# A planned kernel gets new durations, another start of its idle matmuls, a smaller fill of V, and nine of its last residual additions on ScalarE and GpSimd

## The chip, the cores and the metric

The kernel runs on one core of one Trainium2 chip, as one program with one launch. The metric is the device time of that core in microseconds (us); times are medians of several runs. A traced execution also gives the span, from the first to the last instruction, which is a little shorter than its time. The engines are TensorE (PE; its weight loads are listed apart as PEld), VectorE (DVE), ScalarE (ACT), GpSimd (POOL) and SyncE (SP), which here only issues transfers (DMAs).

## What is computed

Four blocks in a row act on a residual stream of 2048 tokens by 512 features, with 32 heads of 16: A, B, A, B, with the same weights for both A and for both B. Each block is `x = x + block(layernorm(x)) @ wo`.

```python
def A(x):                     # causal attention in 4 segments of 512 tokens, with a memory
    for s in range(4):
        p = softmax(q_s @ k_s.T / 4 + causal mask)
        a_mem = phi(q_s) @ M / (phi(q_s) @ z)
        o_s = g * a_mem + (1 - g) * (p @ v_s)
        M, z = M + phi(k_s).T @ v_s, z + sum(phi(k_s))
def B(x):                     # linear attention over all tokens, not causal
    phi_q = concat(softmax(q @ w_phi), softmax(-q @ w_phi))
    phi_k = concat(softmax(k @ w_phi), softmax(-k @ w_phi))
    o = phi_q @ (phi_k.T @ v) / (phi_q @ sum(phi_k))
```

## The kernel before

X, the residual stream, stays in SBUF as 16 tiles of 128 tokens by 512 features, in bf16; so do all weights. A segment, and likewise a chunk of block B, is four tiles. For every segment the kernel does: layernorm (`ln`, statistics by bn_stats and bn_aggr on DVE, the power −1/2 on POOL, L996 to L1006), transposes of the normalized tiles (by DMA from the SP queue, L780, or by PE and a copy, L796, at the start, at the change of layers and at the end), projections (`a_proj`), attention (`a_att`: scores on PE, an exponential of 128x1024 on ACT at L1188, the causal mask on POOL at L1192, PV on PE), output projection and residual (`a_out`, `residual` at L1230), and then the keys and queries of block B for the same tokens (`b_keys`, `b_queries`). Block B's output (`b_out`, L1326) needs all four chunks of its keys, so it comes after the layer's last segment: chunk by chunk between the segments of the next layer, and for the last layer at the very end, where each tile of X goes to HBM as it is done (L1362).

The order of all of this isn't written out by hand. Each step is recorded as an operation (`Program.add`) with its engine or engines to choose from, a cost in us, a latency until others see its result, the operations it depends on, and a priority. `PLAN` (L43 to L180) is a long list that gives every operation its priority by number. `Program.schedule` then plays a clock: at each step it takes, for the engine that can begin first, the ready operation with the lowest priority number, grants it buffers and PSUM banks, and so fixes five queues. `finalize` issues each queue in that order, with waits on semaphores. The chip then runs the five queues in order, with waits only for what an instruction needs. Where the real durations differ from those of the plan, the order stays as planned.

Names and lines that the change and the prediction touch:

- `BEGIN`, `LANDS`, `TO_PE`, `HOP` (L28 to L35): when the engines and loads begin, and how long a result takes to the next engine, in the plan. `BOTH` (L36): the planned time of two score operations that run side by side on different rows of PE. `act_cost` (L730), and the `lat` of `pe`, `act` and `transposed` (L749, L763, L798).
- Idle matmuls (L517 to L551, L578, L1431): where the plan sees a gap on PE, it fills it with matmuls of 128x256 on a tile of zeros, `warm` (filled on DVE at L895), whose results nobody reads. In the plan each lasts 0.108 us, and none begins before 1.5 us. `idle_op` gives each group a dependency on the fill of `warm`.
- `zero_keys` (L953): fills on DVE at the start. Four `Vt` buffers get ones throughout (128x544); V's 16 values per head later overwrite all but every 17th column, which stays one and sums the keys. Four `kt` buffers get zeros.
- The loads at the start: rows of X and halves of WA_k, WA_v, WA_q from the ACT and SP queues, then larger ones from SP (L885 to L951).
- `b_out` with `store` (L1326): per tile a product with Rkv on PE, the denominator and the scaling on DVE (L1345 to L1347), a transposition, the product with `WB_o`, and the residual. In ten of the last sixteen tiles the residual is a DVE addition from PSUM (L1230). In six, named by `TAIL_A` (L1374), PE adds X by a matmul with the identity, and ACT copies the sum to X. `TAIL_T` names the tiles that PE transposes; the others go by a DMA transpose from SP.

Of the kernel before, what the change touches and what calls it, by code (L numbers as in the profile page):

```python
# [8 lines left out]
ALU = mybir.AluOpType  # L9
# [24 lines left out]
BEGIN = 0.75  # L34
LANDS = 2.3  # L35
BOTH = 0.24  # L36
# [212 lines left out]
class Program:  # L249
# [100 lines left out]
    def schedule(self):  # L350
# [137 lines left out]
        while done < n_ops:  # L488
# [26 lines left out]
            (t, _, i, g), e = choice  # L515
            op = ops[i]
            if e == "pe" and self.idle:  # L517
                unit, begin = self.idle[1], self.idle[3]
                recent = [x for x in recent if x[1] > t - WIN]

                def gap(op, t):
# [208 lines left out]
def act_cost(n):  # L730
    return n * 0.000833 + 0.051
# [6 lines left out]
class Kernel:  # L738
# [131 lines left out]
    def gen(self):  # L870
        return self.PS.tile(self.genkind)
# [607 lines left out]
```

## Time and profile before

| what | value |
|---|---|
| median of 3 runs | 515.78 us (515.72, 515.78, 516.08) |
| time of the profiled execution | 514.65 us |
| its span | 512.9 us |
| PE busy, matmuls | 493.3 us (96%), 7314 instructions |
| PEld busy | 304.4 us (59%) |
| DVE busy | 438.2 us (85%), 1026 |
| ACT busy | 436.2 us (85%), 592 |
| POOL busy | 263.1 us (51%), 387 |
| idle matmuls (L1433) | 148, 21.6 us |
| HBM traffic | 6.32 MB read, 2.10 MB written |

A row of a group gives line, engine, operation, output and inputs with their shapes, the count, the total busy time and the mean in ns, and then the idle time of the engine just before it with what ended it. Matmuls overlap: a mean of 380 ns for a 512-wide matmul is its time through the array, while the next one starts about 0.215 us later, so a busy PE isn't PE at its peak, and idle matmuls count as busy. ACT instructions overlap by their ends too: 1078 ns is the mean of the 128x1024 exponential, but they follow each other every 0.92 us.

The span has these stages: the opening to about 20 us; layer 0's four segments, with ACT nearly full, to about 210; the change of layers to about 262, where ACT is at little more than half; layer 1's segments to about 460; and the tail, which has the last keys and queries and the output of the last block B.

### The profile page before, as it was taken

The page shows a single profiled execution, that of the slowest core. Times are in us where ns is not written, and L with a number is a line of the kernel's source. Part 1 is how long each engine was busy: PE and PEld are TensorE (multiplying, and loading weights), DVE is VectorE, ACT ScalarE, POOL GpSimd, SP SyncE. Part 2 cuts the span into 40 slices and gives each one's busy share as a digit, 9 for nine tenths or more (in the row PEclk, how much of TensorE's full clock was granted, in tenths as well). Part 3 has the DMA queues.
Part 4 walks back from the last instruction along what each step waited for, and adds up shares of the span by engine and source line. Part 5 has one row for each costly group of instructions (what it writes and reads, how often), then busy time and mean ns, then how long its engine had stood idle before and what let it go on. Part 6 is the DMA issues. An engine that isn't in the chain of part 4 may idle for free.

```text
span 512.9 us, 17078 instructions
## 1 busy us (share of the span) xinstructions
PE 493.3 (96%) x7314; PEld 304.4 (59%) x7314; DVE 438.2 (85%) x1026; ACT 436.2 (85%) x592; POOL 263.1 (51%) x387
## 2 busy tenths in 40 slices
PE   7999999999999999999999999999999999999997
PEld 6755555665567556657755555565564666565664
DVE  6899789988679978799886998998998678888995
ACT  2999999999999999953599898999999999995433
POOL 4476585545477856240146457565964485732100
DMA  7964423432301311100113534323443222020034
GB/s 250 278 92 79 69 55 52 80 46 43 63 4 26 64 23 23 26 4 4 22 22 65 63 42 87 62 42 60 58 64 63 34 50 38 13 36 5 7 102 123
DMA packets 94539, 29.97 MB, mean 58 GB/s; under 512 B 86272, under 2 KB 94464, under 8 KB 94464
## 3 DMA queue, kind: packets, MB, share of 16 engines
q1 hardware_dynamic: 93216, 27.83, 29.6%
q8 instruction: 58, 0.95, 0.8%
q10 hardware_dynamic: 1248, 1.06, 0.7%
q14 instruction: 17, 0.14, 0.1%
HBM read 6.32 MB, written 2.10 MB: 16 GB/s over the span
## 4 chain that ended last, share of the span: by engine, by line
PE 43%; ACT 41%; DVE 14%; DMA 1%; issue 1%
PE PS L718 39%; ACT PT L1188 32%; ACT Ek L1250 3%; PE PS L1433 3%; ACT phi L1016 2%; DVE stats L996 2%; DVE X L1230 2%; ACT EQ L1299 2%; DVE EQ L1321 1%; PE PS L796 1%; DMA xnT<-xn 1%; DVE O L1347 1%; DVE O L1213 1%; DVE xn L1006 1%; ACT KTo L1299 1%; DVE PhiK L1018 1%
## 5 line engine op out<-in xcount | busy, mean ns | idle before, releaser
L1188 ACT ACTIVATE PT<-PS 128x1024 bf16<-128x1024 f32 x320 | 311.3, 1078 | 12.9 <-PE PS L718 12.2
L1192 POOL TENSOR_SCALAR_AFFINE_SELECT PT<-PT 128x512 bf16<-128x512 bf16 (+2 forms) x280 | 174.6, 635 | 129.6 <-ACT PT L1188 125.8
L718 PEld LDWEIGHTS PS<-VT,PT 128*128 128x128 bf16 x2560 | 75.6, 96 | 19.5 <-POOL PT L1192 2.6
L718 PE MATMUL PS<-VT,PT 128*128 128x17 bf16 x2560 | 82.4, 171 | 1.3 <-DVE stats L996 0.8
L718 PE MATMUL PS<-QT,KT 32*128 32x128 bf16 (+1 forms) x864 | 77.1, 245 | 5.8 <-ACT PT L1188 2.8
L718 PE MATMUL PS<-QT,KTo 32*128 32x128 bf16 (+1 forms) x864 | 75.9, 242 | 2.5 <-ACT PT L1188 1.3
L1255 POOL TENSOR_TENSOR Ek<-Ek,rZ 128x1024 bf16<-128x1024 bf16 x28 | 54.9, 1967 | 37.1 <-DVE rZ L1253 37.0
L718 PEld LDWEIGHTS PS<-QT,KT 32*128 32x128 bf16 x864 | 32.7, 92 | 43.2 <-ACT PT L1188 26.3
L718 PEld LDWEIGHTS PS<-QT,KTo 32*128 32x128 bf16 x864 | 34.9, 93 | 19.8 <-ACT PT L1188 11.7
L1230 DVE TENSOR_TENSOR X<-X,PS 128x512 bf16<-128x512 bf16 x58 | 39.1, 676 | 5.6 <-PE PS L718 5.3
L996 DVE BATCH_NORM_STATS2 stats<-X 128x6 f32<-128x512 bf16 x64 | 43.1, 681 | 0.5
L1250 ACT ACTIVATE Ek<-PS 128x512 bf16<-128x512 f32 x64 | 36.2, 652 | 7.6 <-PE PS L718 7.5
L1251 DVE TENSOR_REDUCE Zk<-Ek 128x64 f32<-128x1024 bf16 x32 | 38.4, 1208 | 3.9 <-ACT Ek L1250 3.6
L1002 POOL TENSOR_TENSOR rstd<-rstd,negh 128x2 f32<-128x2 f32 (+1 forms) x38 | 25.2, 667 | 32.1 <-DVE rstd L1000 30.4
L718 PE MATMUL PS<-xnT,WA_q 128*128 128x128 bf16 x512 | 36.1, 220 | 0.4 <-DVE O L1213 0.4
L718 PE MATMUL PS<-WA_v,xnT 128*128 128x512 bf16 x128 | 36.0, 380 | 0.0
L718 PE MATMUL PS<-WA_k,xnT 128*128 128x512 bf16 x128 | 34.4, 381 | 0.8 <-DVE O L1347 0.4
L718 PEld LDWEIGHTS PS<-xnT,WA_q 128*128 128x128 bf16 x512 | 29.5, 98 | 7.7 <-issue 2.6
L1006 DVE TENSOR_SCALAR xn<-X,mv,rstd 128x512 bf16<-128x512 bf16 x64 | 29.7, 482 | 5.0 <-POOL rstd L1002 4.7
L1213 DVE TENSOR_TENSOR O<-PS,r 128x128 bf16<-128x128 f32 x128 | 31.9, 279 | 1.2
L718 PE MATMUL PS<-WA_o,OT 128*128 128x512 bf16 x128 | 32.5, 380 | 0.1
L718 PE MATMUL PS<-WB_o,OT 128*128 128x512 bf16 x128 | 32.0, 380 | 0.4 <-DVE O L1347 0.3
(132 smaller groups left out, 836.4 us busy)
## 6 DMA issues: line engine op xcount, KB each, us to landing
out_dram<-X SPq DMA_DIRECT2D x16, 128.0 KB, 1.7
X<-in_A_x_dram SPq DMA_DIRECT2D x3, 512.0 KB, 8.6
EQ<-in_B_wqkv_dram SPq DMA_DIRECT2D x2, 512.0 KB, 12.8
OT<-O SPq DMA_TRANSPOSE x46, 2.5
xnT<-xn SPq DMA_TRANSPOSE x36, 2.5
WA_o<-in_A_wo_dram SPq DMA_DIRECT2D x1, 512.0 KB, 10.7
WB_v<-in_B_wqkv_dram SPq DMA_DIRECT2D x1, 512.0 KB, 12.9
WB_o<-in_B_wo_dram SPq DMA_DIRECT2D x1, 512.0 KB, 8.5
```

Of the source, the lines that this page charges most:

```text
L718: return e.matmul(o, l, r, start=st, stop=sp, tile_position=(basep(l), basep(o)))
L996: self.dve(lambda e, t=t: e.bn_stats(self.stats[:, t, :], self.X[:, t, :]), 0.60, [R("X", t)], [R("stats", t)])
L1002: self.pool(lambda e, ve=ve, n=n: e.tensor_tensor(ve, ve, self.negh[:, 0:1].to_broadcast([128, n]), ALU.pow), 0.6, [R("rstd", t0 + i) for ...
L1006: self.dve(lambda e, t=t, xn=xn: e.tensor_scalar(xn.ap[:], self.X[:, t, :], self.mv[:, t, 0:1], self.rstd[:, t:t + 1], op0=ALU.subtract, o ...
L1188: self.act(lambda e, st=st, pt=pt: e.activation(pt.ap[:].rearrange("p b c -> p (b c)"), self.ps[:, st.slot[0] * 512:st.slot[0] * 512 + 102 ...
L1192: self.pool(lambda e, dv=dv, nd=nd: e.affine_select(dv(), dv(), [[0, 2], [0, nd], [1, 128]] if nd > 1 else [[0, 2], [1, 128]], ALU.is_ge, 0.0,
L1213: self.dve(lambda e, r1=r1, view=view, c=c, g=g: e.tensor_tensor(o[c].ap[:, g, :].rearrange("p (h d) -> p h d", d=DH), view()[:, c, :, 0:1 ...
L1230: self.dve(lambda e: e.tensor_tensor(X[:, t, :], X[:, t, :], self.bank(gen), ALU.add), 0.61, [R("X", t), gen()], [R("X", t)])
L1250: self.act(lambda e, sgn=sgn, Ek=Ek, gen=gen: e.activation(Ek.ap[:, sgn, :], self.bank(gen), ACT.Exp, scale=1.0 - 2.0 * sgn), 512, [gen()] ...
L1251: self.dve(lambda e, Ek=Ek, Zk=Zk: e.tensor_reduce(Zk.ap[:], Ek.ap[:].rearrange("p s (h j) -> p s h j", h=H), AX.X, ALU.add), 1.15, [Ek(0) ...
L1255: scale = lambda e, Ek=Ek, rZ=rZ: e.tensor_tensor(Ek.ap[:].rearrange("p s (h j) -> p (s h) j", j=DH), Ek.ap[:].rearrange("p s (h j) -> p ( ...
L1299: self.act(lambda e, sgn=sgn, g=g, gen=gen: e.activation(Eq[sgn].ap[:, g, :], self.bank(gen), ACT.Exp, scale=1.0 - 2.0 * sgn), 512, [gen() ...
```

## The change

The planner's constants and costs are changed, and the list of priorities is a new one of other numbers throughout (not shown). Idle matmuls may begin, in the plan, when the fill of `warm` has ended there, in place of a fixed 1.5 us; and for 3.5 us from then on each counts twice its time. `Vt` is filled in its 17th column alone. In the tail, nine tiles get their residual by an ACT copy from PSUM to a spare `PT` buffer as f32, and a POOL addition to X; DVE keeps six, PE and ACT one.

```diff
-BEGIN = 0.75
+BEGIN = 0.9
+COLD = 3.5
-BOTH = 0.24
+BOTH = 0.27
 PLAN = (
...
-                unit, begin = self.idle[1], self.idle[3]
+                unit, w = self.idle[1], self.idle[2][0]
+                begin = 1e9 if end[w] is None else end[w] + TO_PE["dve"]
+                warmed = begin + COLD
...
-                    return max(0, int((t - at - (SWITCH if op.mode else 0.0) - MARGIN) / unit))
+                    t -= (SWITCH if op.mode else 0.0) + MARGIN
+                    cold = max(0, int((min(t, warmed) - at) / (2 * unit)))
+                    return cold + max(0, int((t - max(at, warmed)) / unit))
+
+                def lasts(at, n):
+
+                    cold = min(n, max(0, int((warmed - at) / (2 * unit))))
+                    return (n + cold) * unit
...
-    return n * 0.000833 + 0.051
+    return n * 0.000833 + 0.063
...
-    def pe(self, mms, reads, writes, pre=(), lat=0.17, cost=None, rows=0):
+    def pe(self, mms, reads, writes, pre=(), lat=0.11, cost=None, rows=0):
...
-        return self.P.add("act", f, act_cost(n), reads, writes, lat=0.13)
+        return self.P.add("act", f, act_cost(n), reads, writes, lat=0.07)
...
-        self.P.add("pe", tr, 0.24, list(reads) + [self.R("ident")], [gen()], lat=0.17, pre=pre)
+        self.P.add("pe", tr, 0.24, list(reads) + [self.R("ident")], [gen()], lat=0.11, pre=pre)
...
-            self.dve(lambda e, b=b: e.memset(b[:], 1.0), 0.25, (), [self.R("vbone")])
+            self.dve(lambda e, b=b: e.memset(b[:, :, 16:17], 1.0), 0.15, (), [self.R("vbone")])
...
-                self.dve(lambda e, b=b: e.memset(b[:], 0.0), 0.25, (), [self.R("ktzero")])
+                self.dve(lambda e, b=b: e.memset(b[:], 0.0), 0.28, (), [self.R("ktzero")])
...
-            self.pool(... ALU.pow), 0.6,
+            self.pool(... ALU.pow), 0.76,
...
-                self.pe(mms, reads, [st()], pre=[pt], lat=0.2, cost=0.23, rows=y + 1)
+                self.pe(mms, reads, [st()], pre=[pt], lat=0.14, cost=0.23, rows=y + 1)
...
-                              0.085 + 0.26 * nd, [pt()], [pt()])
+                              0.176 + 0.23 * nd, [pt()], [pt()])
...
+            elif tt in pool_add:
+                y = self.p_PT.tile()
+                yv = lambda y=y: y.ap[:].rearrange("p a b -> p (a b)").bitcast(F32)
+                self.act(lambda e, yv=yv, gen3=gen3: e.activation(yv(), self.bank(gen3), ACT.Copy), 512, [gen3()], [y()])
+                self.pool(lambda e, yv=yv, t=t: e.tensor_tensor(self.X[:, t, :], self.X[:, t, :], yv(), ALU.add), 1.0, [R("X", t), y()], [R("X", t)])
...
-        TAIL_T, TAIL_A = ((0, 1, 2, 3), (0, 2), (0, 2), (0, 2)), ((3,), (3,), (1, 3), (1, 3))
+        TAIL_T, TAIL_A = ((0, 1, 2, 3), (0, 2), (0, 2), (0, 2)), ((), (), (), (3,))
+        TAIL_P = (1, 3), (1, 2, 3), (1, 2, 3), (1,)
```

As built, the changed kernel's queues stand in another order on every engine. PE's queue begins with 33 idle matmuls in place of 51, then the first transposes, then 8 in place of 6; over the whole kernel there are 131 in place of 148. On DVE's queue the fill of `warm` is fourth in place of sixth. On SP's queue a half of WA_v is ahead of a half of WA_q, and WA_o is ahead of the second segment's rows. Which engine makes a copy out of PSUM changes for some: net, outside the residuals, eight fewer on ACT and eight more on DVE, three of them 256 wide. The last ten of the sixteen outputs stand in one row at the end of SP's queue, in place of the last seven.

More of the change, by code (lines that the diff above doesn't have):

```diff
@@ L544, in schedule @@
                     if banks:
-                        f = self.idle_op(at, n, min(banks)[1])
+                        f = self.idle_op(at, n, min(banks)[1], lasts(at, n))
                         queues[e].append(f.i)
@@ L576, in schedule, with idle_op @@
         return max(end)
-    def idle_op(self, at, n, bank):
-        emit, unit, after, _ = self.idle
+    def idle_op(self, at, n, bank, lasts):
+        emit, unit, after = self.idle
         f = Op()
@@ L583, in idle_op @@
         f.emit = {"pe": lambda e: emit(e, n, bank)}
-        f.cost, f.lat, f.pri, f.weight, f.mode = {"pe": n * unit}, 0.17, 0.0, 1.0, 0
+        f.cost, f.lat, f.pri, f.weight, f.mode = {"pe": lasts}, 0.17, 0.0, 1.0, 0
         f.rows, f.mate = 0, None
@@ L1001, in ln @@
                       [R("mv", t0 + i) for i in range(n)], [R("rstd", t0 + i) for i in range(n)])
-            self.pool(lambda e, ve=ve, n=n: e.tensor_tensor(ve, ve, self.negh[:, 0:1].to_broadcast([128, n]), ALU.pow), 0.6,
+            self.pool(lambda e, ve=ve, n=n: e.tensor_tensor(ve, ve, self.negh[:, 0:1].to_broadcast([128, n]), ALU.pow), 0.76,
                       [R("rstd", t0 + i) for i in range(n)] + [R("negh")], [R("rstd", t0 + i) for i in range(n)])
@@ L1324, in b_queries, with b_out @@
         return Eq, ze
-    def b_out(self, c, Eq, ze, pri0, pri1, store, by_pe=(), add_pe=()):
-        self.P.tag = (self.L, "bout%d" % c)
+    def b_out(self, c, Eq, ze, pri0, pri1, store, by_pe=(), add_pe=(), pool_add=()):
+        self.P.tag = (self.L, ("tail%d" if store else "bout%d") % c)
         R, P = self.R, self.P
@@ L1429, in build @@
                 for c in range(4):
-                    self.b_out(c, *prev[c], base + 90 + c, base + 91 + c, True, by_pe=TAIL_T[c], add_pe=TAIL_A[c])
+                    self.b_out(c, *prev[c], base + 90 + c, base + 91 + c, True, by_pe=TAIL_T[c], add_pe=TAIL_A[c], pool_add=TAIL_P[c])
         def idle(e, n, b):
@@ L1434, in idle @@
             return ins
-        P.idle = (idle, 0.108, [self.R("warm").last_write], 1.5)
+        P.idle = (idle, 0.108, [self.R("warm").last_write])
         P.psum = self.PS
```

272 rows, old and new, of the table PLAN are left out of this document.

## The prediction

> **What bounds the kernel now.** I read the page's chain of waits first, then its first groups, then the opening and the tail in order of time, then busy time by stretch.
>
> The page's chain, by engine:
>
> ```profile
> PE 43%; ACT 41%; DVE 14%; DMA 1%; issue 1%
> ```
>
> PE and ACT take turns in setting the end; a microsecond taken from DVE or POOL is worth little unless it stands in a stage of its own. The busiest group of the page, and the stretches of the two attention stages (columns: stretch, length, then busy us of PE, PEld, DVE, ACT, POOL):
>
> ```profile
> L1188 ACT ACTIVATE PT<-PS 128x1024 bf16<-128x1024 f32 x320 | 311.3, 1078 | 12.9 <-PE PS L718 12.2
> ```
>
> ```profile
> 20.00:200.00 180.00, 174.53 (x2818) 105.52 (x2817) 154.66 (x358) 175.09 (x224) 117.35 (x170) 1.00 0.35 57
> 262.00:460.00 198.00, 191.53 (x3031) 114.27 (x3029) 169.93 (x396) 188.39 (x244) 120.48 (x178) 1.00 0.31 51
> ```
>
> ACT is idle 4.9 us of 180 (2.7%) and 9.6 us of 198 (4.9%): both stages go at ACT's pace, but for these 14.5 us. The opening in order of time (start, us):
>
> ```profile
> 2.85 0.17 DVE L895 MEMSET warm<- 128x128 uint32 x1
> 3.08 7.38 PE L1433 MATMUL PS<-warm 128*128 128x256 bf16 x51 [3.08 <-DVE H8b L907]
> 7.03 0.41 DVE L1006 TENSOR_SCALAR xn<-X,mv,rstd 128x512 bf16<-128x512 bf16 x1
> 10.29 0.39 PE L796 MATMUL PS<-ident,xn 128*128 128x128 bf16 x4
> ...
> 14.01 1.06 PE L718 MATMUL PS<-xnT,WA_q 128*128 128x128 bf16 x16
> ```
>
> This is a stall that PE makes for itself. The first normalized tile is there at 7.44, but the 51 idle matmuls ahead of its transposes last until 10.46. The plan put them from 1.5 on at 0.108 us each, to end at 7.0; they waited for the fill of `warm` (3.02), and went at 4 in 0.5 us until 6.5, the rest at about 0.11 each. The chain of waits begins with this group and goes on over PE's matmuls to 34.3, then over ACT's exponentials; so what is saved here shifts all behind it. What could hold it then are the loads (kind, queue, KB, us to landing):
>
> ```profile
> WA_v<-in_A_wv_dram ACTq DMA_DIRECT2D x1, 256.0 KB, 6.0
> WA_q<-in_A_wq_dram SPq DMA_DIRECT2D x1, 256.0 KB, 7.4
> WA_v<-in_A_wv_dram SPq DMA_DIRECT2D x1, 256.0 KB, 8.6
> WA_q<-in_A_wq_dram ACTq DMA_DIRECT2D x1, 256.0 KB, 8.4
> ```
>
> Issued at 2.21, 2.27, 2.77 and 3.25, they land at 8.2, 9.7, 11.4 and 11.7. The tail, in two stretches (same columns):
>
> ```profile
> 478.00:489.00 11.00, 10.40 (x161) 8.39 (x160) 11.00 (x30) 2.77 (x6) 0.00 (x0) 1.00 0.12 23
> 489.00:510.00 21.00, 21.00 (x178) 12.87 (x178) 18.50 (x45) 7.66 (x13) 0.00 (x0) 1.00 0.41 110
> ```
>
> DVE is full to 489; then PE is, and the chain runs over PE to 510.1, where ACT makes the last tile and its output goes. POOL does nothing.
>
> **The change part by part.**
>
> *Opening: −2.2 us.* V's fill shrinks from 544 to 32 elements (0.51 us each; a 128x32 copy of L925 takes 0.22), and as built only one stands ahead of `warm` in place of two, with two 0.33 us steps of key fills. From 0.91: 0.33 + 0.2 + 0.33, so `warm` begins near 1.8 rather than 2.85 and PE at 2.0. Now 33 idle matmuls follow: 16 in the 3.5 slow us, 17 at 0.11, ending at 7.4. The DVE rows to the first tile don't move: its second bn_stats waits for the second row load (1.24 + 3.6 = 4.9), against 5.23 before, so the tile comes at 7.1 to 7.4. Transposes at 7.4 instead of 10.18: 2.8 us. Of that the loads give back some: the order on SP puts WA_v ahead of WA_q, so V's second half lands about 9.7, Q's about 11.7. After 8 idle matmuls, two transposes, 16 K matmuls and 2 wide ones PE stands at V near 9.9 (not held), and at Q near 11.2, held to 11.7, where before it stood at 14.01: 2.3 us. I take 2.2. Bounds: 2.9 if Q isn't held; 0.5 if the later loads (WA_o now ahead of the next rows on SP, the raw weights) hold the first segment instead. What else moves in SP's queue, the transposes of raw weights and their places among the xnT ones, feeds the second segment, whose first exponentials come some 37 us later (40 tiles at 0.917), and the keys of chunk 0 (58.4). That is the cover.
>
> *Durations and the new order: −0.8 us.* The constants change no instruction, but the order of all five queues and who does a copy. They are nearer to the trace: nine exponentials of the chain take 8.25 us, 0.917 each; planned 0.904, now 0.916. A round from transposes (471.01) over ACT's copy (471.43) to the next matmul (472.11) takes 1.10; the old constants add to 0.24 + 0.20 + 0.478 + 0.29 = 1.21, the new ones to 0.24 + 0.14 + 0.490 + 0.23 = 1.10. That makes the new order likelier to fit; it prices nothing. What can be priced: outside the residuals ACT loses net five 512-wide copies and three 256-wide ones (5 x 0.49 + 3 x 0.28 = 3.3 us; a pair of 512-wide goes by in 0.98), and DVE gets them (5 x 0.61 + 3 x 0.35 = 4.1). By the chain's shares: −3.3 x 0.41 + 4.1 x 0.14 = −0.8. Idle matmuls outside the opening stay (91, then 90). For the bounds: if both attention stages left ACT idle 2.7%, 4.2 us would go; at 4.9% in both, 3.8 would come. I take −0.8, the row nearest to what is known.
>
> *Tail: −1.1 us.* DVE's residuals fall from 10 to 6 (4 x 0.61 = 2.4 us), identity matmuls on PE from 6 to 1 (5 x 0.21 = 1.1 us of the chain's PE). Nine tiles go by an ACT copy (the L774 copies take 0.60, and ACT is busy 7.66 of 21) and a POOL addition. No row shows that addition. Nearest is
>
> ```profile
> L1255 POOL TENSOR_TENSOR Ek<-Ek,rZ 128x1024 bf16<-128x1024 bf16 x28 | 54.9, 1967 | 37.1 <-DVE rZ L1253 37.0
> ```
>
> By elements half of it, 0.98 us; by bytes (3 KB read per partition against 2.25) 2.62. I take the first: it is the same operation, and half as many elements. The added wait: outputs on SP wait for POOL, and all later outputs stand behind. As built, the last 10 outputs follow SP's last transposes, at 0.585 each (7 in 4.09 before), 5.9 us. Take E for the end of PE's last matmul. From the tiles 1 to 3 on, PE still has transposes and matmuls of 6.2 us, so they come near E−5.5 and the last output can go at E+0.7 as it does now. POOL has five additions in that time (tiles 3, 1, 11, 10, 13): at 0.98 they end at E−0.6, unseen; above 1.12 each tenth costs 0.5 us. So only PE's 1.1 us counts. Bounds: −2.5 if the DVE time counts too; +1.0 if the addition takes 1.5 (+1.9, less 1.1, rounded up).
>
> [...]
>
> *Sum.* −2.2 − 0.8 − 1.1 = −4.1. The profiled execution: span 512.9, time 514.65 (1.75 around it). So 510.55 for such an execution; the median shown, 515.78, lies 1.13 above it: **511.7 us**.
>
> **The rivals.**
>
> *The new order fits better than the copies say (0.22).* ACT's idle time falls in both stages to the 2.7% of the first: −4.2 in place of −0.8, so 508.3. For it: the constants that now meet 0.917 and 1.10. Against: by the table of waits PE waits for ACT 109 times before weight loads (41.8 us), and these depend on tiles and banks, not on constants.
>
> *The new order fits worse (0.10).* 4.9% in both: +3.8 in place of −0.8, so 516.3, no change to be told. For it: DVE, full from 230 to 250 (20.0 of 20.0 us), gets two more xnT copies there. Against: these are 1.2 us.
>
> *POOL's additions follow bytes (0.08), slower.* At 2.62 five of them end at 5 x 2.62 − 5.5 = 7.6 behind E, the last outputs 7.5 later: 511.7 + 7.5 = 519.2. It decides from 4.1 us on, so from 1.94 us each. For it: the f32 tile is as large as the 1024-wide bf16 one. Against: that row's broadcast operand shows a cost by element.
>
> *The opening gives nothing (0.10).* The loads of the raw weights and rows take the whole first 20 us (DMA share 0.89): −0.5 in place of −2.2, so 513.4. Against: the four landings above.
>
> **How the numbers follow.** The forecast has 0.50. Repeated measurements of this kernel can tell about 0.2%, 1.0 us. Faster by more: forecast, better fit, opening lost, less 0.05 for what strays out of each: 0.77; within: the worse fit: 0.10; slower: POOL and those 0.05: 0.13. The forecast's own range is 509.5 to 513.5; the better fit pulls down to 507, the worse fit up to 516.6, and POOL by bytes is left out.
>
> **What would show it.** Opening: the first group on `warm` with 33, from about 2.0 to 7.4; transposes at 7.4; the Q matmuls near 11.7; ACT's first exponential at 18.5 rather than 20.65. Middle: nine exponentials still 8.25, ACT idle near 2.7% and 4.9%. Tail: POOL's rows on X near 1.0 us, the last instruction an ACT copy to X, seven or more outputs at 0.585 without a gap. The prediction is wrong if the opening's lead is gone by 100 us, or if POOL's X rows exceed 1.9.

## The result and the profile after

The changed kernel takes **520.00 us** (median of 20 runs, 516.88 to 522.71); the kernel before, run beside it, 515.87. The ratio is 1.0075, 95% interval 1.0058 to 1.0091: 0.75% slower, where 511.7 was forecast. The times are spread over 6 us, and they go with the mean granted clock that each execution records:

| mean clock of the execution | executions of 20 | median us |
|---|---|---|
| 0.999 to 1.0 | 3 | 517.06 |
| 0.996 to 0.997 | 4 | 519.02 |
| 0.983 to 0.990 | 13 | 520.89 |

In the 122 executions of the kernel before that ran beside the experiments, the lowest mean clock is 0.993. So two things are to be explained: some 1.4 us at the full clock (the changed kernel's five such executions, with those of a second series below, have a median of 517.0 us, the kernel before 515.2 to 515.7), and 2 to 4 us more where the clock falls. The profiled execution (517.06 us, span 515.3) has the full clock throughout, so it shows the first alone. Its span is 2.4 us longer than that of the profile before, since that one (514.65 us) is among the faster of its kernel; differences of about 1 us between two traces are within what one kernel shows (executions of the kernel before at the full clock have spans of 512.5 to 514.4 us). Its chain and its busiest group:

```profile
PE 57%; ACT 25%; DVE 10%; DMA 5%; issue 1%; SPq 1%; POOL 0%
...
L1198 ACT ACTIVATE PT<-PS 128x1024 bf16<-128x1024 f32 x320 | 309.0, 1049 | 12.2 <-PE PS L728 11.2
```

ACT's share of the chain fell from 41% to 25%; PE has it now, and transfers (DMA) went from 1% to 5%. The exponentials themselves cost no more (1049 ns against 1078). By stretches (length, then busy us of PE, PEld, DVE, ACT, POOL):

```profile
20.00:200.00 180.00, 170.89 (x2717) 103.12 (x2715) 152.91 (x349) 172.32 (x219) 114.29 (x168) 1.00 0.35 56
262.00:460.00 198.00, 192.12 (x3006) 115.54 (x3006) 167.16 (x392) 189.11 (x244) 120.26 (x175) 1.00 0.31 50
...
489.00:510.00 21.00, 20.83 (x204) 13.46 (x204) 19.12 (x48) 9.66 (x18) 8.43 (x8) 1.00 0.36 94
```

In the first attention stage ACT is idle 7.7 us instead of 4.9; in the second 8.9 instead of 9.6. The opening in order of time did much of what was forecast:

```profile
1.77 5.37 PE L1449 MATMUL PS<-warm 128*128 128x256 bf16 x33 [1.77 <-DVE warm L905]
...
7.17 0.40 PE L806 MATMUL PS<-ident,xn 128*128 128x128 bf16 x4
...
12.22 0.55 PE L728 MATMUL PS<-xnT,WA_q 128*128 128x128 bf16 x7 [0.64 <-DMA WA_q<-in_A_wq_dram]
```

The clearest view of where the time goes is the start of the exponential with a given number (counted from 0 to 319; there are 320), from each trace:

| exponential | before | after, full clock | difference |
|---|---|---|---|
| 0 | 20.6 | 17.3 | −3.4 |
| 10 | 31.7 | 31.1 | −0.6 |
| 20 | 44.1 | 42.4 | −1.7 |
| 30 | 53.6 | 54.1 | +0.5 |
| 40 | 65.6 | 68.9 | +3.3 |
| 160 | 258.9 | 262.6 | +3.8 |
| 319 | 459.1 | 464.2 | +5.1 |
| end of the span | 512.9 | 515.3 | +2.4 |

The opening gains 3.4 us, the part from the last exponential on gains 2.7 (51.1 instead of 53.8). Between them 8.5 us are lost, 6.7 of these before number 40, in the stretch from 17 to 69 us. Number 10 is not a fair mark: between numbers 0 and 10 ACT now does seven other operations, where it did four, and by number 20 the lead is 1.7 again.

Of the 2.7 us at the end, 0.9 go with a late transposition in the trace before, for which PE waits:

```profile
462.53 1.02 PE L718 MATMUL PS<-WB_k,xnT 128*128 128x512 bf16 x4 [0.75 <-DMA xnT<-xn]
```

That transposition landed 4.71 us after its issue. In the two traces below that have the short opening and the old tail it landed after 3.14 and 3.18 us, and the part from the last exponential on took 52.9 us.

In the stretch from 17 to 69 us the table of waits of the changed kernel's trace (17 to 70 us; us in total, times, longest) names transpositions that SyncE's queue issues. OT<-EQ turns B's raw weights, which are then folded by products on PE; xnT<-xn turns normalized rows; EQ<-xn turns those for B's keys. In the kernel before, PE waited 0.4 us for OT<-EQ in 17 to 45 us:

```profile
DVE xn L1016 <- DMA xnT<-xn: 1.9, 4, 0.8
...
PEld PS L728 <- DMA EQ<-xn: 1.5, 1, 1.5
PE PS L728 <- DMA OT<-EQ: 1.4, 1, 1.4
...
PE PS L728 <- DMA EQ<-xn: 1.1, 1, 1.1
```

SyncE's queue in that stretch (start, length; a length is the time that the issuing takes):

```profile
5.02 2.73 SPq L792 DMA_DIRECT2D EQ<-in_B_wqkv_dram  x1
7.79 4.46 SPq L792 DMA_DIRECT2D WB_v<-in_B_wqkv_dram  x1
12.29 2.88 SPq L792 DMA_DIRECT2D X<-in_A_x_dram  x2
15.21 1.42 SPq L792 DMA_DIRECT2D wphi<-in_B_w_phi_dram  x1
16.68 2.14 SPq L792 DMA_DIRECT2D WB_o<-in_B_wo_dram  x1
18.86 7.45 SPq L790 DMA_TRANSPOSE OT<-EQ  x4
...
32.90 3.54 SPq L790 DMA_TRANSPOSE OT<-EQ  x2
```

The first issues took about 0.5 us each, as the planner counts for every load; from 5.02 on they take 1.4 to 4.5, until 18.8. Then a transposition goes every 1.3 us or slower, one right behind the other. The last two of the eight OT<-EQ are issued from 32.90 on, and the first of them, the seventh, lands at 36.24. PE stands at its product from 34.94 to 36.38. In the kernel before, the last three OT<-EQ and the first EQ<-xn are issued so:

```profile
31.07 3.99 SPq L780 DMA_TRANSPOSE OT<-EQ  x3
...
52.37 1.26 SPq L780 DMA_TRANSPOSE EQ<-xn  x1
```

There the seventh is issued at 32.38 and lands at 35.59.

### The profile page after: what moved, and what is told of

Its sections match the earlier page's. It is cut to its first block, busy times and chain, and to the rows that moved or that the text cites. A ratio compares the mean times of both kernels' runs of the same rounds, so it can differ in the third digit from the quotient of the medians.

```text
span 515.3 us, 17036 instructions
## 1 busy us (share of the span) xinstructions
PE 493.3 (96%) x7292; PEld 304.6 (59%) x7292; DVE 437.1 (85%) x1030; ACT 438.2 (85%) x588; POOL 271.9 (53%) x396
## 4 chain that ended last, share of the span: by engine, by line
PE 57%; ACT 25%; DVE 10%; DMA 5%; issue 1%; SPq 1%; POOL 0%
PE PS L728 55%; ACT PT L1198 19%; DMA X<-in_A_x_dram 2%; ACT Ek L1260 2%; DVE stats L1006 1%; PE PS L1449 1%; DMA xnT<-xn 1%; ACT EQ L1309 1%; ACT phi L1026 1%; PE PS L806 1%; DVE X L1240 1%; DVE PhiK L1028 1%; DVE xn L1016 1%; DMA OT<-EQ 1%; DVE VT L784 1%
## 5 line engine op out<-in xcount | busy, mean ns | idle before, releaser
L1198 ACT ACTIVATE PT<-PS 128x1024 bf16<-128x1024 f32 x320 | 309.0, 1049 | 12.2 <-PE PS L728 11.2
L1202 POOL TENSOR_SCALAR_AFFINE_SELECT PT<-PT 128x512 bf16<-128x512 bf16 (+2 forms) x280 | 172.3, 627 | 122.1 <-ACT PT L1198 118.7
L728 PEld LDWEIGHTS PS<-VT,PT 128*128 128x128 bf16 x2560 | 78.2, 96 | 22.9 <-issue 4.0
L728 PE MATMUL PS<-VT,PT 128*128 128x17 bf16 x2560 | 86.2, 171 | 1.0 <-DVE X L1240 0.5
L728 PEld LDWEIGHTS PS<-QT,KTo 32*128 32x128 bf16 x864 | 35.2, 93 | 18.8 <-ACT PT L1198 10.6
L1012 POOL TENSOR_TENSOR rstd<-rstd,negh 128x2 f32<-128x2 f32 (+1 forms) x38 | 26.8, 708 | 34.6 <-DVE rstd L1010 33.2
L1240 DVE TENSOR_TENSOR X<-X,PS 128x512 bf16<-128x512 bf16 x54 | 36.6, 679 | 9.4 <-PE PS L728 9.0
L1016 DVE TENSOR_SCALAR xn<-X,mv,rstd 128x512 bf16<-128x512 bf16 x64 | 27.8, 441 | 3.7 <-DMA xnT<-xn 1.9
```

The costliest lines, as they stand in the source:

```text
L728: return e.matmul(o, l, r, start=st, stop=sp, tile_position=(basep(l), basep(o)))
L1012: self.pool(lambda e, ve=ve, n=n: e.tensor_tensor(ve, ve, self.negh[:, 0:1].to_broadcast([128, n]), ALU.pow), 0.76, [R("rstd", t0 + i) for ...
L1016: self.dve(lambda e, t=t, xn=xn: e.tensor_scalar(xn.ap[:], self.X[:, t, :], self.mv[:, t, 0:1], self.rstd[:, t:t + 1], op0=ALU.subtract, o ...
L1198: self.act(lambda e, st=st, pt=pt: e.activation(pt.ap[:].rearrange("p b c -> p (b c)"), self.ps[:, st.slot[0] * 512:st.slot[0] * 512 + 102 ...
L1202: self.pool(lambda e, dv=dv, nd=nd: e.affine_select(dv(), dv(), [[0, 2], [0, nd], [1, 128]] if nd > 1 else [[0, 2], [1, 128]], ALU.is_ge, 0.0,
L1240: self.dve(lambda e: e.tensor_tensor(X[:, t, :], X[:, t, :], self.bank(gen), ALU.add), 0.61, [R("X", t), gen()], [R("X", t)])
```

## The experiments

Eighteen runs follow. Medians of the kernel before, run beside them, are 515.5 to 515.9. "Full clock" below means executions with a mean clock of 0.999 or more.

### Where the clock falls

**The changed kernel again**, for a trace with a dip.

> The changed kernel once more, for its time and for a trace of an execution in which the granted clock dips; nothing is left out. Theory A (the clock is lost where TensorE is starved by the new order of its work, 35 to 66 us): if the mean granted clock of the profiled execution is below 1.0, the dip lies in 30 to 100 us. Rival B (the shorter idle groups of the opening, 33 instead of 51): the dip lies before 30 us. Rival C (the last stage, where VectorE is relieved): it lies behind 460 us. By all of them the time is 517 to 521 us, 1.006 to 1.010 of the kernel before.

518.87 us (9 runs); seven executions have 0.983 to 0.990. The profiled one (520.34 us, clock 0.986) has one stretch at half clock, from 36.8 to 50.4 us; exponential 40 starts at 72.6 instead of 68.9. Just before, in order of time on PE, the wait is longer than the 1.44 us of the first profile:

```profile
37.42 1.33 PE L728 MATMUL PS<-O,OT 128*128 128x128 bf16 x11 [2.10 <-DMA OT<-EQ]
```

PE's busy time around that place in stretches of 2 us (length, busy us of PE first; the granted clock is the third value from the end). The trace with the dip:

```profile
34.00:36.00 2.00, 1.16 (x23) 0.67 (x22) 2.00 (x7) 1.96 (x4) 1.67 (x3) 1.00 0.65 28
36.00:38.00 2.00, 0.58 (x6) 0.61 (x7) 0.40 (x2) 0.84 (x1) 1.31 (x3) 0.69 0.66 128
38.00:40.00 2.00, 1.67 (x14) 0.85 (x12) 1.79 (x3) 0.56 (x1) 0.00 (x0) 0.50 0.36 69
...
50.00:52.00 2.00, 2.00 (x37) 1.25 (x34) 1.15 (x3) 1.85 (x3) 0.68 (x1) 0.90 0.61 118
```

and the first profile of the changed kernel, which has none:

```profile
34.00:36.00 2.00, 0.84 (x18) 0.45 (x16) 2.00 (x5) 1.96 (x3) 2.00 (x4) 1.00 0.47 66
36.00:38.00 2.00, 1.60 (x18) 0.91 (x18) 1.22 (x3) 0.88 (x2) 0.93 (x2) 1.00 0.46 89
```

From 34 to 38 us PE is busy 1.74 of 4 us in the trace with the dip and 2.44 in the other. Two more traces below have half clock from about 37 or 38 us on and little work for PE in the same 4 us: 1.27 (VectorE relieved) and 1.81 (another order of five transpositions). Busy time alone doesn't decide. With three loads later in SyncE's queue (below), the clock falls between 32 and 36 us (0.73 there, 0.50 in the next 4 us), although PE is busy 3.58 us from 28 to 32 and 2.98 from 32 to 36; PE doesn't wait for OT<-EQ there, but 0.42 and 0.68 us for other engines. In the first profile of the changed kernel PE is busy 2.66 of 4 us from 58 to 62, and the clock stays at 1.00. That the wait's length differs from run to run (1.44 and 2.10 us in these two traces) fits the spread of the times. Theory A's place was right; whether the wait causes it is the next run.

**The wait filled.** Idle matmuls ahead of the product that waits:

```diff
+            if e == "pe" and i == 441 and self.idle:
+                banks = [(tile_free(h), b) for b, h in enumerate(self.psum.holder)]
+                banks = [x for x in banks if x[0] is not None and x[0] + TO_PE["act"] <= t]
+                f = self.idle_op(t, 12, min(banks)[1], 0.0)
+                queues[e].append(f.i)
+                end.append(t)
             commit(i, e, t, g)
```

> The changed kernel with one group of 12 idle matmuls (about 1.3 us at full clock) ahead of the matmul of the folded weights that waits for the transposition OT<-EQ at 35 us; nothing is left out, all queues keep their order. Theory A (the clock falls to half at 37 us because TensorE, waiting for that transposition, is idle for 1.4 to 2.1 us): the wait is now filled, the dip from 37 to 50 us is gone from nearly all executions (mean clock 0.997 to 1.0), and the median falls from about 519.5 to 516.5 to 517.5. Rival (the dip has other causes, such as the sum of the idle time from 20 to 37 us): most executions still show 0.983 to 0.990 and the median stays at 518.5 to 520.

516.96 us (12 runs, ratio to the kernel before 1.0018, interval 1.0004 to 1.0032). Two executions have 0.996, ten 0.999 to 1.0, none less. The place of the wait now:

```profile
34.00:36.00 2.00, 1.40 (x26) 0.78 (x24) 2.00 (x7) 1.96 (x4) 1.55 (x3) 1.00 0.73 96
36.00:38.00 2.00, 2.00 (x26) 1.77 (x26) 0.89 (x3) 0.95 (x2) 1.43 (x3) 1.00 0.56 105
```

Twelve matmuls that compute nothing take 2 to 3 us off the median, and the executions at 0.983 to 0.990, 20 of 29 in the two series without them, are gone. Theory A holds for this long dip: PE's wait for OT<-EQ makes it. It doesn't hold for every dip, as the next run says.

**The long idle group given back.**

```diff
-        f.emit = {"pe": lambda e: emit(e, n, bank)}
+        shown = 51 if n == 33 else n
+        f.emit = {"pe": lambda e: emit(e, shown, bank)}
```

> The changed kernel with 51 idle matmuls in its first group instead of 33, which takes the lead of the opening away (18 more at 0.11 us each); nothing else differs. Theory A with theory 2 (the lead only makes TensorE arrive earlier at a transposition that lands at 36 to 37 us in any case; its wait there is what lets the clock fall): the first exponential starts about 2 us later than 17.3, TensorE's wait at 35 us is below 0.5 us, the clock stays at 0.996 to 1.0 in most executions, and the median falls from 518.9 to 516.5 to 517.5, although TensorE is given 2 us more of idle work. Rival (the dip comes from the new order whatever the opening does): the clock dips to 0.983 to 0.990 in most executions, and the median is 519 to 521.

519.70 us (6 runs): a miss; the rival's clock and time came true. Four executions have 0.986 to 0.990. In the profiled one PE no longer waits for OT<-EQ, and the drop there shrinks: its page has the clock at 8 tenths from 26 to 39 us and 9 from 39 to 52, where the page of the changed kernel again has 9 and 5. But it has 7 from 325 to 338 us, where no other page read has less than 9, and 8 from 468 to 481 (so have the one with three loads later, from 467 on, and the kernel before with the new tail and its own numbers, from 463 on). What makes those was not found.

### Where the opening's lead goes

**The kernel before with a short opening** (its first group emitted as 24 in place of 51).

> The kernel before with one edit: its first idle group has 24 matmuls instead of 51, as if it were planned for the cold clock; list, prices and tail stay the old ones. Theory 1 (the lead of the opening is carried to the end, and the new order is what loses it): the first exponential starts about 3 us earlier, the lead is still over 2 us at the 160th exponential, and the time falls to 512.5 to 514. Rival 2 (the stage behind the opening is set by SyncE's queue, which still issues loads until 19 us and a transposition every 1.3 us after it): the first exponential starts 3 us earlier, the lead is below 1 us by the 40th exponential, and the time stays at 515 to 516.5. For the clock: if the short opening alone is what makes the granted clock dip, several of the executions show a mean below 0.999; if not, none does.

515.60 us (12 runs), ratio 1.0003, interval 0.9983 to 1.0023. Exponential 0 starts at 19.0 instead of 20.6 (1.6 us, where 3 were expected), number 10 at 30.0 instead of 31.7, number 20 at 44.0 against 44.1, and the last at 458.9 against 459.1. Rival 2 holds: with the old list too, the lead is gone by 44 us. What the old list loses it to can be read from the chain of that trace, where the chain of the kernel before had only PE and ACT (start, us, what):

```profile
32.59 3.58 DMA OT<-EQ
```

The median hides a second thing. Eight of the twelve executions have a clock below 0.999 (0.990 to 0.997), against 6 of 22 of the kernel before beside them; the four at the full clock have a median of 514.27, 1.4 us less than the kernel before. In the profiled one (span 1.0 us shorter) 0.9 of that lie behind the last exponential, at the transposition near 462 us that lands sooner. Whether the short opening lowers the clock, and why that landing differs, was not followed up.

Three kernels ask what holds that place: SyncE's loads, or VectorE, which is busy without a gap from 16 to 32 us in the changed kernel.

**Three loads later in SyncE's queue** (WB_v, the last rows of X, WB_o), behind the first four OT<-EQ:

```diff
+        sp = P.queues["sp"]
+        first = (17, 12, 433, 443, 432, 431, 16, 18, 19)
+        sp[9:9+len(first)] = first
```

> The changed kernel with three loads (B's weights for V, the last four row tiles of X, B's output weights) behind the first four transpositions OT<-EQ in SyncE's queue; nothing is left out. Theory 2 (after the opening SyncE's queue sets the pace: its loads hold the first transposition until 18.9 us): the first OT<-EQ starts by 17 us instead of 18.9, the transpositions up to 40 us land 1.5 to 2 us earlier, and the 40th exponential comes 1 to 2 us earlier than in the changed kernel (68.9 us), the time 1 to 2 us lower at the same clock. Rival 1 (the order of the list, not the queue): the transpositions come earlier, but the 40th exponential stays within 0.4 us of 68.9 and the time within 0.5 us.

518.57 us, 516.3 and 517.0 at the full clock: nothing gained, where theory 2 expected 1 to 2 us. The first OT<-EQ starts at 16.81, but the moved loads now stand ahead of the other four, and the seventh lands at 36.98. That points to the seventh landing, not the first.

**VectorE relieved** (statistics over 128 of the 512 columns, so this kernel leaves out three quarters of each row there):

```diff
-                self.dve(lambda e, t=t: e.bn_stats(self.stats[:, t, :], self.X[:, t, :]), 0.60, ...
+                self.dve(lambda e, t=t: e.bn_stats(self.stats[:, t, :], self.X[:, t, 0:part]), 0.60, ...
```

> The changed kernel, with the statistics of A's layer norm of row tiles 4 to 15 in the first layer taken over 128 of the 512 columns (12 instructions of VectorE, 0.60 us each by the trace, become shorter; their mean and variance are over a quarter of the row). Theory 3 (from 15 to 35 us VectorE, busy without a gap, is the bound that eats the lead of the opening): VectorE has some 4 us less to do by 40 us, the 20th exponential starts 1.5 to 4 us earlier than in the changed kernel at full clock (42.4 us) and the time is 1.5 to 4 us lower at the same clock. Theory 2 (SyncE's queue, with the landing of the last OT<-EQ at 36 us, sets it): that landing stays within 0.5 us of 36.2 and the 20th exponential within 0.7 us of 42.4, the time within 0.7 us at the same clock.

519.29 us; 515.9 and 516.9 at the full clock, against 516.2 and 517.0 for the changed kernel in its second series. VectorE is busy 13.75 us from 16 to 32 instead of 15.99. The seventh OT<-EQ lands at 37.01, PE goes on at 37.14, and from 34 to 38 us it is busy 1.27 of 4 us, the least of the traces compared above. Theory 3 falls: VectorE is busy, but it isn't the bound.

**Two loads behind all eight OT<-EQ** (WB_v and WB_o), in the changed kernel:

```diff
+        first = (17, 18, 12, 433, 443, 432, 431, 345, 445, 347, 444, 355, 434, 446, 16, 19)
+        sp[9:9+len(first)] = first
```

> The changed kernel with the two loads of B's weights that nothing needs before 50 us (for V and for the output) behind all eight transpositions OT<-EQ in SyncE's queue, instead of ahead of them; nothing is left out. Theory 2 (SyncE's queue, not VectorE and not the order of the list, sets the pace from 17 to 37 us; these two issues hold it for 6.6 us in the trace of the changed kernel, of which the landing of the raw weights at 18.7 us hides some): the seventh OT<-EQ lands 1 to 3 us before 36.2, TensorE's wait for it (1.44 us) goes, the clock stays at 0.996 to 1.0 without an added idle matmul, and the time is 515 to 516.5, half a us to 2 below the changed kernel with the filled wait (516.96). Rival (VectorE or the list's order): the landing comes earlier, but the time at full clock stays at 516.5 to 517.5.

The seventh is issued at 30.60 and lands at 33.10, PE's wait for it is gone, and exponential 40 starts at 67.5 instead of 68.9:

```profile
16.44 6.60 SPq L790 DMA_TRANSPOSE OT<-EQ  x4
...
30.60 2.58 SPq L790 DMA_TRANSPOSE OT<-EQ  x2
33.22 2.11 SPq L792 DMA_DIRECT2D WB_v<-in_B_wqkv_dram  x1
35.38 0.51 SPq L792 DMA_DIRECT2D WB_o<-in_B_wo_dram  x1
```

The median is 517.35, though, above the expected 515 to 516.5: four of twelve executions still have 0.990, and no trace shows where. At the full clock it is 516.24. With the wait filled as well:

> The changed kernel with both edits: the filled wait (12 idle matmuls) and the two loads of B's weights behind the transpositions OT<-EQ. Theory A (what is left of the dips in the kernel with the late loads comes from the same place, 33 to 37 us): the clock stays at 0.996 to 1.0 in nearly all executions, and the median falls from 517.35 to 515 to 516.3. Rival (those dips lie elsewhere): some executions still show 0.990, and the median stays at 516.5 to 517.5.

518.04 us (9 runs), above what both theories expected; one execution at 0.990, five at 0.996 to 0.997, 516.82 at the full clock. That is not below the filled wait alone: the two edits don't add up.

**The same two loads, in the kernel before with the short opening:**

> The kernel before with the short opening (24 idle matmuls instead of 51) and the same two loads behind the transpositions OT<-EQ. Theory 2: the lead of the opening, gone by the 20th exponential in the kernel with the short opening alone, is now kept in part: 0.7 to 2 us at the 40th exponential, and the time falls to 513.5 to 515. Rival: no lead is left at the 40th exponential (within 0.4 us), time 515 to 516.

513.66 us (12 runs), ratio 0.9973, interval 0.9960 to 0.9987. Exponential 20 starts at 42.8 (44.0 without the moved loads), number 40 at 64.4 (65.5), number 160 at 257.9 (258.7). So theory 2 is shown for the old list: the lead is lost to SyncE's queue, and 1.2 of its 1.6 us are kept up to number 40 once two loads stand behind the transpositions. At the full clock the gain over the short opening alone is 0.65 us (513.62 against 514.27); the rest of the median's 1.9 goes with the clock, below 0.999 in 2 of 12 executions here.

### Where the new order loses 3 us more

From 54 to 69 us the changed kernel loses 2.8 us at the full clock. The chain there (start, us, what):

```profile
49.46 4.67 DMA xnT<-xn
...
54.16 0.41 DVE xn L1016
...
59.82 2.49 DMA EQ<-xn
...
62.36 2.45 PE PS L728 x10
```

Two readings: VectorE stands at an xn whose buffer is still being transposed, or PE waits for EQ<-xn, the input of B's keys, which lands at 62.31 (54.92 before). The new list has more xnT ahead of it in SyncE's queue.

**Another order of five transpositions alone.**

> The changed kernel with five transpositions of SyncE's queue in another order: the first layer's KTo and both EQ<-xn go ahead of the second xnT of the last segment (the old order had them so); nothing is left out. Theory 2b (between 42 and 69 us the new order puts transpositions that are not yet needed ahead of EQ<-xn, and TensorE waits at 60 to 63 us): EQ<-xn lands some 2.5 us earlier than 62.3, TensorE's wait there goes, and the 40th exponential comes 1 to 2.5 us earlier than 68.9 at full clock, the time 1 to 2.5 us lower at the same clock. Rival (the order of TensorE's own work there loses it): the 40th exponential stays within 0.5 us and so does the time.

522.52 us (6 runs, all at 0.983 to 0.990). EQ<-xn lands at 63.20: its xn was itself late. Nothing is told apart.

**Six buffers for xn**, with the filled wait:

```diff
+        self.p_xn.bufs = self.p_xn.bufs + self.more.bufs
+        mine = [t for i in P.queues["dve"] for t in P.ops[i].tiles if t.pool is self.p_xn]
+        for k, t in enumerate(mine):
+            t.slot = k % 6
+            t.before = set(mine[k - 6].ops) if k >= 6 else set()
```

> The changed kernel with the filled wait (12 idle matmuls, as before), and six buffers instead of three for the normalised rows xn; the planner still plans with three, so every queue keeps its order and only the waits for a free buffer go. Theory 4 (the 3 us that the new order loses between 54 and 69 us at full clock are VectorE standing at an xn whose buffer waits for a transposition in SyncE's backlog, with what TensorE needs behind it in VectorE's queue): VectorE's waits of xn for xnT<-xn (1.9 us in 17 to 100 us) go, the 40th exponential comes 1 to 3 us earlier than the 69.1 us of the kernel with the filled wait, and the time falls from 516.96 to 514 to 516. Rival (TensorE's waits for EQ<-xn, which lands at 62 us by SyncE's order, are what costs): EQ<-xn lands within 0.5 us of 62 to 63, the 40th exponential stays within 0.5 us, and so does the time.

517.68 us against 516.96 without. VectorE's waits are gone, EQ<-xn lands at 62.33, exponential 40 starts at 68.9. Theory 4 falls.

**The same, with KTo and both EQ<-xn ahead of two xnT:**

```diff
+        first = (381, 462, 464, 1164, 1162)
+        sp[35:35+len(first)] = first
```

> The changed kernel with the filled wait and six buffers for xn (517.68), and in SyncE's queue the first layer's KTo and both EQ<-xn ahead of the two last xnT of the last segment. Theory 5 (the 3 us lost between 54 and 69 us are TensorE waiting for EQ<-xn, held in SyncE's queue behind transpositions that are needed later; the earlier try of this order could not show it, since its xn waited for buffers and the clock had dipped): EQ<-xn lands 2 to 3.5 us earlier than 62.3, TensorE's waits for it (1.2 and 0.9 us) go, the 40th exponential comes 1.5 to 3 us earlier than 68.9, and the time is 515 to 516.3. Rival (the order of TensorE's and VectorE's own work loses it): EQ<-xn lands earlier, but the 40th exponential stays within 0.7 us of 68.9 and the time within 0.7 us of 517.68.

515.86 us (12 runs; ratio 1.0005, interval 0.9990 to 1.0020), 1.8 below the kernel with the six buffers. EQ<-xn is issued 3.7 us earlier, its rows land at 60.01 and 60.48, and PE's waits for it are gone:

```profile
54.45 1.26 SPq L796 DMA_TRANSPOSE KTo<-ktoko  x1
56.08 1.19 SPq L796 DMA_TRANSPOSE EQ<-xn  x1
57.60 1.75 SPq L796 DMA_TRANSPOSE EQ<-xnb  x1
```

Exponential 40 starts at 67.7 and number 90 at 125.1, where the kernel before has 125.2. Theory 5 holds; its gain is 1.2 us at number 40, a little below what it expected, and 2.3 from number 60 on.

**All of it together.**

> The same kernel with the two loads of B's weights behind the transpositions OT<-EQ as well: the changed kernel with every wait that SyncE's queue was seen to make between 17 and 69 us shortened. Theory 2 with 5 (SyncE's queue is where the forecast's 8 us were lost): 513.5 to 515, below the kernel before (515.8) though not below the mix of three edits on the kernel before (512.49). Rival (the order of the list itself costs as much): 516 to 518.

515.74 us: nothing more from the two loads, between what the two theories expected. By exponential 90 it is level with the kernel before (125.1 and 125.2); it is 1.5 us behind at number 160, level once more at 240 (359.9 and 359.7), and 3.0 us behind at the last one (462.1 and 459.1). These 3 us of the new order, all lost behind 360 us, were not taken apart.

### The tail

**The changed kernel with the old tail.**

> The changed kernel with the old tail: the nine last additions are VectorE's and TensorE's again, with the numbers of the list as the changed kernel has them (the nine entries of ScalarE's copies left out); all before the tail is the same. Theory: the new tail is a gain of 2 to 3 us at full clock, so this kernel is 2 to 3 us above the changed one with the same clock (518 to 521 for executions at clock 1.0, about 522 as a median). Rival: the tail's gain is the 1.1 us that was forecast, then 517 to 519 at full clock. Rival C on the clock (the dips are made by the new tail): no execution shows a mean clock below 0.999, and the median falls to about 518 or lower; by theory A and rival B the clock dips in most executions as in the changed kernel (0.983 to 0.997).

521.06 us (4 runs, all at 0.987). From the last exponential to the end it takes 52.8 us, against 51.1 in both profiles with the new tail: 1.7 us for the new tail within the same list. No execution of it is at the full clock, so the drop isn't the new tail's.

**The kernel before with the new tail,** numbers taken over from the old list:

> The kernel before with the new tail alone: the nine last additions by ScalarE's copies and GpSimd, the old list (each copy placed half a number ahead of its addition), the old prices and the old opening. Theory (the tail is worth 1.5 to 2.7 us by itself): 513 to 514.3 us, with GpSimd's additions at 1.1 to 1.2 us each and the end after the last exponential at 51 to 52.3 us instead of 53.8. Rival (the tail gains only with the order of the new list, or its forecast 1.1 us): 514.5 to 516.

520.03 us: it loses 4.2 (ratio 1.0083). Up to the last exponential it is the kernel before (459.0); from there it takes 58.7 us. GpSimd's additions cost 1.16 us as in the changed kernel, so the loss isn't in their length; the next run says that it is in the order. **With numbers searched for it:**

> The kernel before with the new tail alone, as in the earlier run of it, but with the numbers of the list for the last stage adapted to the new tail by a search over the planner's own model; prices and the order up to the last stage are the old ones. Theory (the tail is worth 1.5 to 2.7 us, but only with an order that fits it): 513 to 514.5 us, and the end comes 51 to 52.5 us after the last exponential instead of 53.8. Rival (ScalarE's copies and GpSimd's additions cost more than they free, and what the changed kernel gained in its tail came from elsewhere in the list): 515 to 518.

514.89 us (12 runs), ratio 0.9993, interval 0.9976 to 1.0010; 514.13 at the full clock against 515.22. The median is not told from no change, and lies between the two expectations; at the full clock it is 1.1 us less. The profiled execution has a lower clock from 463 to 475 us (8 tenths in its page), so its 54.4 us from the last exponential on say nothing. The tail is a loss with an order that doesn't fit and about 1 us of gain with one that does, less than the theory's 1.5.

### What adds up

**The short opening, the two loads and the new tail, in the kernel before.**

> The kernel before with three edits at once: the short opening (24 idle matmuls), the two loads of B's weights behind the transpositions OT<-EQ, and the new tail with the numbers searched for it; the old list and prices up to the last stage. Theory (these gains lie in different stages and add up): 1.8 us from the first two (513.66 against 515.48) and 0.6 to 1.5 from the tail, so 512.2 to 513.2, less than both kernels. Rival (the last stage takes back what comes early): 513.2 to 514.5.

512.49 us (511.56 to 513.49, 6 runs), ratio **0.9931**, interval 0.9911 to 0.9952: less than both kernels, all executions at 1.0. From the last exponential on it takes 52.2 us, against 52.9 with the short opening and the old tail. With six buffers for xn:

> The kernel of the three edits, with six buffers for xn instead of three and all queues in the same order. Theory 4 (waits for xn's buffer cost where the queue of SyncE is behind): in the old order that wait hardly occurs in 17 to 100 us, so the time stays within 0.5 us of the kernel without it. Rival (the wait costs in later segments too): 0.5 to 2 us less.

513.11 us (12 runs), 512.55 at the full clock: no gain from the buffers.

## Why the prediction was wrong

*The opening: right in what happens, wrong in what it is worth.* The idle group ends at 7.14 (7.4 forecast), the first transposes stand at 7.17, Q at 12.22 with a wait of 0.64 for its load (11.7 forecast, held), the first exponential at 17.27 (18.5). The lead is 3.4 us, more than the 2.2, and partly by luck: Q came 1.8 us sooner (14.01 before), not 2.3, and the other 1.6 us arose between Q and the first exponential, which the sum didn't price. (The idle matmuls before 6.5 us were read as 4 in 0.5 us; the trace has one every 0.213 us, which is the 16 in 3.5 us that the sum uses.) **The step that failed is the sentence that named the cover**: "What else moves in SP's queue, the transposes of raw weights and their places among the xnT ones, feeds the second segment, whose first exponentials come some 37 us later". The exponentials did come later; but PE works through its queue in order, and products of those transposes (the folding of B's weights) stand in it at 35 us, with the first segment's scores behind them. The seventh landing is set by SyncE's queue and did not move with the opening (35.59 before, 36.17 with the old list and the short opening, 36.24 after). "What is saved here shifts all behind it" was said of PE's own work, with only the loads of the first segment looked at as a limit. The run of the old list with the short opening shows it without the new order, and the one with the two loads moved shows the cause.

*Durations and the new order: mis-sized, outside its bounds.* The term was −0.8 with bounds of −4.2 and +3.8. Between the two profiles, with the opening's 3.4 us used up, it is +5.1 at the last exponential. With the opening at nothing and the tail at −2.7 that makes the 2.4 us of the spans. Of the 5.1, 2.5 come back by moving five entries in SyncE's queue (464.7 to 462.2 at the last exponential, both with six buffers); about 3 us stay without a cause. The term was priced by copies moved between ACT and DVE. What decided the part that was found is the order in SyncE's queue, which I had called moved and then counted at nothing. The 0.585 us of an output was the only price of a SyncE issue in the sum; the rows of the trace before already showed 1.3 us for each transposition and 4.3 for the issue of WB_v.

*In all.* From the forecast −4.1 to the +2.4 us between the two profiles it takes +2.2 for the opening, +5.9 for the new order and −1.6 for the tail. The falling clock adds about 3 us to the median.

*The tail: right in sign.* POOL's additions take 1.16 us each, between the two bounds and near the 0.98 taken:

```profile
496.37 1.16 POOL L1372 TENSOR_TENSOR X<-X,PT 128x512 bf16<-128x512 bf16 x1 [16.20 <-ACT PT L1371]
497.70 3.40 POOL L1372 TENSOR_TENSOR X<-X,PT 128x512 bf16<-128x512 bf16 x3 [0.18 <-ACT PT L1371]
506.00 4.71 POOL L1372 TENSOR_TENSOR X<-X,PT 128x512 bf16<-128x512 bf16 x4 [4.89 <-ACT PT L1371]
```

The gain is 2.7 us between the two profiles, 0.9 of them the late landing in the trace before; 1.7 within the new list, and about 1.1 with the old one. Within the new list that is more than the 1.1 that was forecast; that DVE's relief makes the rest, as the bound of −2.5 had it, is not shown.

*The rivals.* None of them was what happened. "The opening gives nothing" was the nearest, but it put the limit at the loads of the first 20 us. "The new order fits worse" had 3.8 at most, and it looked for DVE at 230 to 250 us. That PE, waiting, would lose its clock (3 us of the median, by the filled wait) was no rival at all, though the kernel spends its idle matmuls on just that: the planner fills only gaps that it foresees, and by its own clock it issued the seventh OT<-EQ at 28.4 us, the chip at 32.9.

*The test named in advance* ("wrong if the opening's lead is gone by 100 us") was met: it is gone by 54.

## What to carry to other kernels

A gain at the start of a kernel is worth only what the next resource lets through: follow it, queue by queue, to the first landing that doesn't move with it, and count every issue in a DMA queue at its measured length (0.5 to 4.5 us on SyncE's here). A new order should be judged by what stands behind each wait in each queue, since a few entries decide more than all the copies together. Where PE fills foreseen gaps to keep its clock, an unforeseen wait can cost more than the wait itself (here, with 2.10 us in place of 1.44, half clock from 38 to 50 us, and exponential 40 came 3.7 us later); a dozen idle matmuls ahead of an uncertain landing were a cheap cover (2 to 3 us off the median).

## What the runs showed of the hardware

- In five profiled executions of the changed kernel and its variants the granted clock was near half from 39 to 52 us (5 tenths in the page). In the changed kernel again it was 0.50 from 38 to 50 us, although PE was busy 11.34 of these 12 us. Around its start, at 36.8, PE waited 2.10 us and was busy 1.74 of the 4 us from 34 to 38. With a wait of 1.44 us (2.44 of the same 4 us), and with the wait filled (3.40), the clock stayed at 1.00. PE's busy time alone doesn't explain the drops: with three loads later the clock fell although PE was busy 3.58 of the 4 us from 28 and 2.98 of the next 4, and in the first profile it stayed at 1.00 from 58 to 62 us with 2.66 of 4.
- Issuing a transfer held SyncE's queue for far longer than 0.5 us: 4.46 us for the 512 KB of WB_v at 7.79 us, while earlier loads were on their way; moved to 33.22 it took 2.11, and WB_o 0.51 instead of 2.14.
